# First batch of an attention, gated-MLP and expert kernel: three split products become one fp32 product, values before u, and the weights are split behind the norm

## The chip, the cores and the metric

The kernel runs on one core of a Trainium2 chip. The metric is the time of one execution on the device in microseconds; three runs of the kernel before gave 959.96, 960.23 and 961.21 us, the median is 960.23 us. The engines are TensorE (PE, whose weight loads are a row of their own, PEld), VectorE (DVE), ScalarE (ACT), GpSimd (POOL) and SyncE (SP, which here only issues DMA).

## The reference

Three layers stand one behind the other, for 8 batches of 576 rows: attention over keys and values that are averaged in groups of 8, a gated MLP, and two of four small attention experts for each row. The change touches the first batch of the first two. Cut to these:

```python
k_p = k.reshape(B, H, 72, 8, D).mean(axis=3)
v_p = v.reshape(B, H, 72, 8, D).mean(axis=3)
attn = softmax(q @ k_p.T / sqrt(D))
x = (attn @ v_p)                          # 8 heads side by side: 576 x 512
h = gelu(x @ w_in)                        # w_in: 512 x 1024
u, v = h[..., :512], h[..., 512:]
v_n = (v - mean(v)) / sqrt(var(v) + 1e-06) * g_ln
v_s = w_sg @ v_n + b_sg                   # over the 576 rows
x2 = x + (u * v_s) @ w_out
```

The weights w_in and w_out and all else are float32 in the reference; the kernel gets these two as pairs of 32-bit words of a 64-bit number, which it turns into float32 on the chip.

## The kernel before

The program has two phases, each a class. Phase A (`PhaseA`) does attention and gated MLP and stores x2 to DRAM in two parts, a high and a low one; phase B does the experts. The work of phase A goes batch by batch. Each batch has these steps: pooling of k and v (`pool_k`, `pool_v`), scores in five tiles of 128 rows (`score`), exponentials (`probs`), scaling by the sum (`finish`), transposes of the probabilities (`trans`), attention times values (`av`), copies of x out of PSUM (`put_x`), the v half of the MLP (`vpart`, in the first batch `vfirst` and one `vpart` for the last 64 rows), the norm of v (`norm`), the u half (`upart`, four blocks of 128), the spatial product over the rows (`spatial`, four blocks, each followed by the gate u * v_s) and the output product (`outp`, four blocks, which end in x2h and x2l and their stores).

Most products are made of three: both operands are split into a high part (float32r, a rounded float32) and a low part, and the sum is high x high + high x low + low x high. The scores and the transposes are plain float32 products (on PE they show as two records each for a product). The high parts are copies on ACT, the low parts subtractions on DVE or POOL.

The first batch also loads the weights. `load64` turns a staged block of w_in (`load_wi`, 8 blocks: parts 0 are u, parts 1 are v) or w_out (`load_wo`, 4 blocks) into a high and a low part, with two instructions on ACT and six on DVE (L124 to L130). The order of the first batch is written by hand: `SEQ` is a string of step names, and `first` calls them in this order (W and a number is `load_wi`, U is `upart`, Y is `vfirst`, V the last `vpart`, N the norm, S the spatial weights, O `load_wo`, P `spatial`; C, X and F are score, probabilities and scaling of the second batch, k its key pooling, v its value pooling). A scheduler below may interleave what is independent. Tables give the engine: `FD` lists the tiles (batch, tile) whose scaling runs on DVE, the others run on POOL; `SE` says for four spatial weight blocks whether D (DVE) or P (POOL) makes the low part. The output products of batch b are interleaved with the transposes of batch b + 1, and `av` of b + 1 follows them; behind it batch b + 1 begins with `vpart`.

Buffers are shared by tag: "raw" has three buffers, through which k, v and the staged w_out blocks go; "x2" has four, for the temporary tiles of `load64` and for x2h and x2l; "mm" has two PSUM buffers, for most products; "xg" has one, for the parts of x and then of the gate.

## Time and profile before

| what | value |
|---|---|
| median of three runs | 960.23 us |
| span of the profiled execution | 958.4 us |
| what the median run has more than the profiled span | 1.8 us |
| PE busy | 912.3 us (95%) |
| DVE busy | 693.4 us (72%) |
| ACT busy | 517.4 us (54%) |
| POOL busy | 445.2 us (46%) |
| PE busy from 132 us to the end | 813 of 826 us |
| second batch's first value product starts | 133.23 us |

The span runs from the first to the last instruction of the profiled execution; the profile gives no other time of it. Matmuls are pipelined: a record lasts longer than its distance from the next one, so prices on PE are read from start to start.

### The profile page before, as it was taken

How to read it: one execution, taken by the hardware profiler on the slowest of the kernel's cores; microseconds unless marked ns; L12 is line 12 of the kernel's file. 1: busy time of each engine (PE TensorE's matmuls, PEld its weight loads, DVE VectorE, ACT ScalarE, POOL GpSimd, SP SyncE). 2: the span in 40 equal slices, each digit the busy share in tenths (PEclk: the TensorE clock that was granted, in tenths of full speed). 3: DMA queues.
4: the chain of work that ended last, by engine and by line, in shares of the span. 5: the costliest groups of instructions: out<-in, count | busy, mean ns of one | idle time of the engine just before them, and what ended most of it. 6: DMA issues, size and time to landing. Idle time of an engine off the chain costs nothing.

```text
span 958.4 us, 18444 instructions
## 1 busy us (share of the span) xinstructions
PE 912.3 (95%) x6488; PEld 864.5 (90%) x6488; DVE 693.4 (72%) x1876; ACT 517.4 (54%) x1285; POOL 445.2 (46%) x621
## 2 busy tenths in 40 slices
PE   4897789999999999999999999899999999999997
PEld 4677769989989999899899899899999999999987
DVE  6998838667667577586576614897879797878785
ACT  3765324344343443343443433777777776877776
POOL 6554737658369368376583560122222222323221
PEclk9798989999999999999999999999999999999999
DMA  9601522312412404223116014425353534435121
GB/s 321 246 13 44 170 106 68 137 62 72 148 35 72 171 12 142 101 64 140 58 54 193 26 40 135 141 49 166 85 165 91 160 97 133 134 93 165 50 62 75
DMA packets 51644, 102.86 MB, mean 107 GB/s; under 512 B 10592, under 2 KB 16736, under 8 KB 50656
## 3 DMA queue, kind: packets, MB, share of 16 engines
q1 hardware_dynamic: 51408, 101.68, 33.1%
q8 instruction: 52, 0.85, 0.4%
q14 instruction: 40, 0.33, 0.1%
q10 hardware_dynamic: 144, 0.00, 0.0%
HBM read 59.72 MB, written 28.31 MB: 92 GB/s over the span
## 4 chain that ended last, share of the span: by engine, by line
PE 75%; DVE 14%; ACT 4%; issue 3%; DMA 2%; SPq 1%; POOL 1%; ACTq 0%; DVEq 0%; POOLq 0%
PE sc L224 4%; PE av L911 4%; PE op L457 3%; PE sp L433 3%; PE sp L434 3%; PE sp L432 3%; PE up L416 3%; PE up L418 3%; PE up L417 3%; PE op L458 3%; PE op L459 3%; PE vp L355 3%; PE vp L356 3%; PE vp L357 3%; PE t L891 2%
## 5 line engine op out<-in xcount | busy, mean ns | idle before, releaser
L865 POOL TENSOR_SCALAR pr<-pr,sm,gw 128x128 f32<-128x128 f32 (+3 forms) x119 | 72.2, 608 | 209.6 <-DVE sm L861 137.6
L849 ACT ACTIVATE pr<-s,sm 128x256 f32<-128x256 f32 (+4 forms) x160 | 83.0, 520 | 41.3 <-DVE sm L846 19.5
L432 PE MATMUL sp<-wsh,vnh 128*128 128x288 f32 x256 | 78.7, 308 | 3.9 <-ACT vnh L400 3.9
L457 PE MATMUL op<-g,woh 128*128 128x288 f32 x256 | 77.3, 306 | 3.9 <-DVE x2l L464 3.1
L416 PE MATMUL up<-x,wih 128*128 128x288 f32 x256 | 76.9, 300 | 1.4 <-ACT xu L324 1.4
L458 PE MATMUL op<-g,woh 128*128 128x288 f32 x256 | 76.2, 298 | 1.4 <-DVE g L445 1.4
L433 PE MATMUL sp<-wsh,vnl 128*128 128x288 f32 x256 | 76.9, 300 | 0.6 <-DVE vnl L402 0.6
L434 PE MATMUL sp<-wsl,vnh 128*128 128x288 f32 x256 | 76.8, 300 | 0.0
L418 PE MATMUL up<-x,wil 128*128 128x288 f32 x256 | 75.9, 296 | 0.7 <-DVE wil L130 0.7
L720 PE MATMUL pj<-xbh,wql 128*128 128x288 f32 x256 | 75.5, 295 | 0.0
L718 PE MATMUL pj<-xbh,wqh 128*128 128x288 f32 x256 | 75.5, 295 | 0.0
L719 PE MATMUL pj<-xbl,wqh 128*128 128x288 f32 x256 | 75.5, 295 | 0.0
L417 PE MATMUL up<-x,wih 128*128 128x288 f32 x256 | 75.1, 293 | 0.0
L459 PE MATMUL op<-g,wol 128*128 128x288 f32 x256 | 74.2, 295 | 0.0
L846 DVE CUSTOM_DVE_ANT_0 s<-s,mk 128x512 f32<-128x512 f32 (+3 forms) x128 | 62.3, 487 | 3.2 <-PE t L891 2.9
L896 DVE TENSOR_TENSOR pbl<-t,pbh 128x512 fp32r<-128x512 f32 (+3 forms) x128 | 60.4, 484 | 2.5 <-ACT pbh L895 0.9
L224 PE MATMUL sc<-kbd,qt 128*128 128x144 f32 (+1 forms) x320 | 50.7, 306 | 11.8 <-DMA qt<-q_in 8.3
L891 PE MATMUL t<-ident,pr 128*128 128x128 f32 x320 | 56.3, 277 | 3.3 <-POOL pr L865 3.1
L911 PE MATMUL av<-pbh,vt 128*128 128x320 f32 (+4 forms) x224 | 55.9, 279 | 2.7 <-ACT pbh L895 2.7
L224 PEld LDWEIGHTS sc<-kbd,qt 128*128 128x128 f32 (+1 forms) x320 | 44.7, 193 | 14.7 <-issue 11.1
L464 POOL TENSOR_TENSOR x2l<-x2l,x2h 128x576 fp32r<-128x576 f32 x8 | 11.4, 1428 | 99.1 <-ACT x2h L463 99.1
L400 ACT ACTIVATE vnh<-vg,rs 128x512 fp32r<-128x512 f32 (+1 forms) x40 | 27.2, 718 | 53.1 <-POOL rs L392 40.4
(247 smaller groups left out, 3352.1 us busy)
## 6 DMA issues: line engine op xcount, KB each, us to landing
kraw<-k_in SPq DMA_DIRECT2D x16, 576.0 KB, 3.8
x<-x2h SPq DMA_DIRECT2D x32, 288.0 KB, 2.1
x<-x2l SPq DMA_DIRECT2D x32, 288.0 KB, 2.1
xbl<-x SPq DMA_DIRECT2D x32, 288.0 KB, 4.1
xbh<-x SPq DMA_DIRECT2D x32, 288.0 KB, 3.9
kd<-scr SPq DMA_DIRECT2D x64, 144.0 KB, 2.5
out<-o SPq DMA_DIRECT2D x32, 288.0 KB, 4.1
vraw<-v_in SPq DMA_DIRECT2D x16, 512.0 KB, 4.0
```

The costliest lines, as they stand in the source:

```text
L224: nc.tensor.matmul(ps[:m, p // 2, (p % 2) * 144:(p % 2) * 144 + 144], qt[:, p, o:o + m], kbd[:, p, :], start=p % 2 == 0, stop=True, skip_g ...
L416: nc.tensor.matmul(o, self.wi[0][:, kc, c], xh, start=kc == 0, stop=False)
L417: nc.tensor.matmul(o, self.wi[0][:, kc, c], xl, start=False, stop=False)
L418: self.upmm = nc.tensor.matmul(o, self.wi[1][:, kc, c], xh, start=False, stop=kc == 3).ins
L432: nc.tensor.matmul(o, vh[:, k, c], self.ws[0][:, k, s], start=k == 0, stop=False)
L433: nc.tensor.matmul(o, vl[:, k, c], self.ws[0][:, k, s], start=False, stop=False)
L434: nc.tensor.matmul(o, vh[:, k, c], self.ws[1][:, k, s], start=False, stop=False)
L457: nc.tensor.matmul(o, self.wo[0][:, k, c], gh[:, s], start=k == 0, stop=False)
L458: nc.tensor.matmul(o, self.wo[0][:, k, c], gl[:, s], start=False, stop=False)
L459: self.opmm = nc.tensor.matmul(o, self.wo[1][:, k, c], gh[:, s], start=False, stop=k == 3).ins
L849: nc.scalar.activation(pt[:, s], o, AF.Exp, bias=st[:, 0:1], scale=-1.0, accum_out=st[:, 1 + 4 * j:2 + 4 * j])
L911: nc.tensor.matmul(ps[:, s - lo:], vt[:, j, 2 * p + e].rearrange("p a d -> p (a d)"), t[:, e, j * PTS + s:j * PTS + up], start=j == 0 and ...
```

## The change

In the first batch alone, x, v and u are computed by one float32 product each in place of three products of parts. The pooled v is kept as one float32 tile `v32` (in the buffer of the high part), the transposed probabilities as one tile, and x only as `XU` (no high or low part). `load64` now gives one float32 block, with one ACT instruction and three on DVE (L131 to L133). The second batch and later ones need the parts of w_in, so a new step D (`split_wi`: a copy on ACT, a subtraction on DVE) makes them behind the products' own loads and ahead of the norm in the list; for w_out the split stands inside `load_wo`. `parts_v` makes the two part tiles of v when the second batch pools. In `SEQ` the v weights and products (W4 Y0 to W7 Y3, V4) now stand ahead of the u ones (W0 U0 and on), and their staging h2 h3 ahead of h0 h1. `FD` gets three more tiles of the second batch, `SE` is all DVE, and two low parts of the gate go from POOL to DVE.

```diff
-FD = {(0, 0), (0, 1), (1, 3), (1, 4)}
+FD = {(0, 0), (0, 1), (1, 0), (1, 1), (1, 2), (1, 3), (1, 4)}
-SE = 'PDPP'
+SE = 'DDDD'
-       "s4 e4 f4 y0 y1 y2 t0 t1 t2 t3 t4 z l W0 U0 W1 U1 W2 U2 K Q k o0 o1 W4 Y0 W5 Y1 W6 Y2 W7 Y3 S2 S1 S0 "
-       "V4 W3 N0 U3 S4 N2 S5 N4 S3 C0 C1 o2 O0 P0 C2 X0 X1 F0 o3 O1 P1 C3 F1 X2 O2 R P2 F2 X3 O3 "
+       "f4 y0 y1 y2 t0 t1 t2 t3 t4 z l W4 Y0 W5 Y1 W6 Y2 W7 Y3 V4 W0 U0 W1 U1 N0 W2 U2 K Q k o0 o1 W3 "
+       "U3 N2 N4 S2 S1 S0 S4 S5 D4 D5 D6 D7 D0 D1 D2 D3 S3 C0 C1 o2 O0 P0 C2 X0 X1 F0 o3 O1 P1 C3 F1 X2 "
...
-        nc.scalar.activation(gf, zf, AF.Copy, scale=2.0 ** -112)
-        nc.vector.tensor_scalar(g, g, 3, 0x7FFFF000, op0=OP.logical_shift_left, op1=OP.bitwise_and)
-        nc.vector.scalar_tensor_tensor(a, zh, 0x80000000, g, op0=OP.bitwise_and, op1=OP.bitwise_or)
-        nc.scalar.activation(hi, a.bitcast(F32), AF.Copy)
-        nc.vector.tensor_scalar(g, a, 0xFF800000, None, op0=OP.bitwise_and)
-        nc.vector.tensor_scalar(zh, zh, 0x1FF, None, op0=OP.bitwise_and)
-        nc.vector.scalar_tensor_tensor(lf, zh, 2.0 ** 32, zl, op0=OP.mult, op1=OP.add)
-        nc.vector.scalar_tensor_tensor(lo, lf, 2.0 ** -52, gf, op0=OP.mult, op1=OP.mult)
+        nc.scalar.activation(g.bitcast(F32), zh.bitcast(F32), AF.Copy, scale=2.0 ** -112)
+        nc.vector.tensor_scalar(g, g, 3, None, op0=OP.logical_shift_left)
+        nc.vector.scalar_tensor_tensor(g, zl, 29, g, op0=OP.logical_shift_right, op1=OP.bitwise_or)
+        nc.vector.scalar_tensor_tensor(out.bitcast(U32), zh, 0x80000000, g, op0=OP.bitwise_and, op1=OP.bitwise_or)
+
+    def split(self, src, hi, lo, eng=None):
+        self.nc.scalar.activation(hi, src, AF.Copy)
+        (eng or self.nc.vector).tensor_sub(lo, src, hi.bitcast(F32))
...
         nc.scalar.activation(hi[:, :, o:o + m], ps[:, :, :m], AF.Copy)
+        if b == 0:
+            return
         nc.vector.tensor_sub(lo[:, 0:4, o:o + m], ps[:, 0:4, :m], hi[:, 0:4, o:o + m].bitcast(F32))
...
+            self.X32[b, p] = self.XU[b][:, p * S:p * S + S].rearrange("p (a n) -> p a n", a=2)
+            nc.scalar.activation(self.X32[b, p], ps[:, :, :HS], AF.Copy)
+            return
...
-            nc.tensor.matmul(ps, xh, wh, start=kc == 0, stop=False)
-            nc.tensor.matmul(ps, xl, wh, start=False, stop=False)
-            nc.tensor.matmul(ps, xh, wl, start=False, stop=kc == 3)
+            nc.tensor.matmul(ps, self.XU[0][:, o:o + 128], self.w32[:, kc, 512:], start=kc == 0, stop=kc == 3)
...
+                if b == 0:
+                    self.upmm = nc.tensor.matmul(o, self.w32[:, kc, c], self.X32[b, kc][:, h], start=kc == 0, stop=kc == 3).ins
+                    continue
...
-        eng = nc.vector if d >= (3 if b else 2) else nc.gpsimd
+        eng = nc.gpsimd if b and d < 3 else nc.vector
```

On PE, the first batch had its u products first (`up`, L416 to L418) and then the v products (`vp`, L371 to L373). Six rows where the one passes into the other:

```order
L416 MATMUL up<-x,wih 128x288
L417 MATMUL up<-x,wih 128x288
L418 MATMUL up<-x,wil 128x288
L371 MATMUL vp<-wih,x 128x512
L372 MATMUL vp<-wih,x 128x512
L373 MATMUL vp<-wil,x 128x512
```

On PE now, from the first batch's attention times values (`av`; the rows with `vl` are the narrow ones of the last 8 pooled keys) to the second batch's second score group (`sc`):

```order
L340 MATMUL av<-pth,v_99 128x288
L334 MATMUL av<-pth,vl_244 128x288 x7
L340 MATMUL av<-pth,v_99 128x288 x6
L417 MATMUL vp<-w_73,xu 128x512 x16
L256 MATMUL sc<-kbd,qt 128x144 x4
L386 MATMUL vp<-w_73,xu 64x512 x4
L460 MATMUL up<-xu,w_73 128x288 x32
L256 MATMUL sc<-kbd,qt 128x144 x4
```

The v products have moved ahead of all u products, each is one product, and the score groups have moved to either side of the u products.

On ACT now, around the last u blocks (`xu<-up` is a u block's gelu, `e,st<-sc,st` an exponential piece of the second batch's first tile):

```order
L467 ACTIVATE xu<-up 128x576
L266 ACT_TABLE_LOAD
L266 ACTIVATE e,st<-sc,st 128x72 x7
L467 ACT_TABLE_LOAD
L467 ACTIVATE xu<-up 128x576
L266 ACT_TABLE_LOAD
L266 ACTIVATE e,st<-sc,st 128x72
L136 ACTIVATE woh<-w_616 128x4x128
L467 ACT_TABLE_LOAD
L467 ACTIVATE xu<-up 128x576
L130 ACTIVATE g_681<-st_547 128x512
L277 ACT_TABLE_LOAD
```

Before, the four gelus of u stood ahead of the exponentials, with one table load between them; now the exponentials stand among them, with five.

On DVE now, behind the wait for those exponentials (`P` is the scaling of the second batch's first tile, `wol` the low part of an output weight block, `xu<-sp,xu` the gate product, `g<-xu,g` its low part):

```order
L286 RECIPROCAL st<-st 128x8
L289 TENSOR_TENSOR P<-e,st 128x512
L292 TENSOR_TENSOR P<-e,st 128x4x16 x2
L261 TENSOR_REDUCE st<-sc 128x8
L137 TENSOR_TENSOR wol<-w_616,woh 128x4x128
L269 TENSOR_TENSOR e<-sc,st 128x576
L131 TENSOR_SCALAR g_681<-g_681 128x512
L132 SCALAR_TENSOR_TENSOR g_681<-st_547,g_681 128x512
L133 SCALAR_TENSOR_TENSOR w_680<-st_547,g_681 128x512
L485 TENSOR_TENSOR xu<-sp,xu 128x576
L284 TENSOR_REDUCE st<-e 128x8
L261 TENSOR_REDUCE st<-sc 128x8
```

The scaling `P`, which was POOL's, now stands at the head of this stretch, ahead of the first gate product.

## Rows read from the trace of the kernel before

**Rows 1.** The page, part 1: busy us, share of the span, instructions

```profile
PE 912.3 (95%) x6488; PEld 864.5 (90%) x6488; DVE 693.4 (72%) x1876; ACT 517.4 (54%) x1285; POOL 445.2 (46%) x621
```

**Rows 2.** Stretches: us, busy us of each engine (instructions), granted clock, DMA share, GB/s

```profile
39.50:77.00 37.50, 31.13 (x180) 26.92 (x179) 35.43 (x66) 24.82 (x39) 16.25 (x9) 1.00 0.17 54
77.00:84.00 7.00, 6.31 (x25) 5.97 (x26) 5.84 (x13) 5.14 (x19) 0.00 (x0) 0.52 0.05 12
84.00:124.00 40.00, 30.50 (x223) 28.73 (x221) 32.80 (x59) 16.10 (x50) 27.11 (x36) 1.00 0.46 159
124.00:132.00 8.00, 7.44 (x36) 5.80 (x37) 2.58 (x7) 2.02 (x4) 1.98 (x2) 0.57 0.39 150
132.00:958.00 826.00, 813.20 (x5929) 778.03 (x5927) 586.58 (x1674) 451.96 (x1109) 371.34 (x523) 1.00 0.31 98
```

**Rows 3.** PE in order of time: start, us, instruction, idle before and releaser

```profile
41.77 0.40 PE L416 MATMUL up<-x,wih 128*128 128x288 f32 x1 [1.36 <-ACT xu L324]
...
51.39 0.39 PE L371 MATMUL vp<-wih,x 128*128 128x512 f32 x1
...
62.53 0.39 PE L344 MATMUL vp<-wih,x 128*128 128x512 f32 x1
...
76.39 0.53 PE L432 MATMUL sp<-wsh,vnh 128*128 128x288 f32 x2 [3.44 <-ACT vnh L400]
...
133.23 0.39 PE L355 MATMUL vp<-wih,x 128*128 128x512 f32 x1
```

**Rows 4.** The first scores on PE, and two pieces of the chain that ended last

```profile
15.26 5.29 PE L224 MATMUL sc<-kbd,qt 128*128 128x144 f32 x24 [1.69 <-issue]
...
15.26 4.18 PE sc L224 x16
...
85.76 0.99 PE sc L224 x8
```

**Rows 5.** DVE in order of time: one weight block after another

```profile
42.60 0.69 DVE L125 SCALAR_TENSOR_TENSOR a<-st,g 128x512 uint32<-128x512 uint32 x1
43.21 0.68 DVE L130 SCALAR_TENSOR_TENSOR wil<-st,g 128x512 fp32r<-128x512 f32 x1
...
44.48 0.42 DVE L124 TENSOR_SCALAR g<-g 128x512 uint32<-128x512 uint32 x1
44.82 0.68 DVE L129 SCALAR_TENSOR_TENSOR st<-st 128x512 f32<-128x512 uint32 x1
45.42 0.68 DVE L125 SCALAR_TENSOR_TENSOR a<-st,g 128x512 uint32<-128x512 uint32 x1
```

**Rows 6.** DVE by line, 20 to 106 us: busy us, mean ns, idle before

```profile
L277 DVE TENSOR_TENSOR ptl<-tr,pth 128x512 fp32r<-128x512 f32 (+1 forms) x5 | 3.1, 614 | 0.0
L321 DVE TENSOR_TENSOR x<-av,x 128x576 fp32r<-128x576 f32 x4 | 3.0, 750 | 0.3 <-ACT x L320 0.2
```

**Rows 7.** ACT in order of time: the table load ahead of the exponentials

```profile
79.89 1.28 ACT L234 ACT_TABLE_LOAD   x1
```

**Rows 8.** DVE in order of time, 84 to 106 us

```profile
84.47 0.76 DVE L438 TENSOR_TENSOR xu<-sp,xu 128x576 f32<-128x576 f32 x1 [1.56 <-PE sp L436]
...
103.09 1.48 DVE L257 TENSOR_TENSOR P<-e,st 128x512 f32<-128x512 f32 x1
104.50 1.27 DVE L445 TENSOR_TENSOR g<-xu,g 128x576 fp32r<-128x576 f32 x1
```

**Rows 9.** One stretch, columns as in group 2

```profile
85.00:105.00 20.00, 17.27 (x125) 15.94 (x123) 19.68 (x36) 11.56 (x43) 17.86 (x20) 1.00 0.21 73
```

**Rows 10.** The DMA queue and ACT in order of time, 115 to 123 us

```profile
115.35 0.33 SPq L71 DMA_DIRECT2D vraw<-v_in  x1
115.73 0.50 SPq L466 DMA_DIRECT2D x<-x2h  x1
...
122.69 0.65 ACT L463 ACTIVATE x2h<-op 128x576 fp32r<-128x576 f32 x1 [4.26 <-DMA x<-x2h]
```

**Rows 11.** Weight loads by line, 130 us to the end: busy us, mean ns

```profile
L416 PEld LDWEIGHTS up<-x,wih 128*128 128x128 f32 x224 | 42.2, 188 | 0.8
```

More of the change, by code (lines that the diff above doesn't have):

```diff
@@ L83, in consts @@
         nc.scalar.dma_start(self.cm, self.ins["cm"])
[L84 removed]
+        self.kbd, self.v32 = [], []
         for i in range(1):
[L86 to L88 removed]
+            for n, tag, sh in (("kbd", "kbd0", [128, NP, 144]), ("v32", "vhi0", [128, NP, 128])):
+                t = c.tile(sh, F32, tag=tag, name=n)
+                nc.gpsimd.memset(t, 0.0)
                 getattr(self, n).append(t)
@@ L96, in consts, with parts_v @@
         nc.gpsimd.memset(self.vn2[64:66].bitcast(F32), 1.0)
+    def parts_v(self):
+        self.vhi, self.vlo = [], []
+        for l in (self.vhi, self.vlo):
+            n = "vhi0" if l is self.vhi else "vlo0"
+            t = self.c.tile([128, NP, 128], F32R, tag=n, name=n)
+            self.nc.gpsimd.memset(t.bitcast(F32), 0.0)
+            l.append(t)
     def load_gln(self):
@@ L145, in load_wi, with split_wi @@
         k, s = self.wi_cols(part, i)
-        self.load64(self.STG.pop((part, i)), self.wi[0][:, k, s], self.wi[1][:, k, s])
+        self.load64(self.STG.pop((part, i)), self.w32[:, k, s])
+    def split_wi(self, part, i):
+        k, s = self.wi_cols(part, i)
+        self.split(self.w32[:, k, s], self.wi[0][:, k, s], self.wi[1][:, k, s])
     def stage_wo(self, f):
@@ L184, in pool_v @@
         raw = self.RAW["v", b]
+        if b == 0:
+            v = self.v32[0]
+            for i in parts:
+                t = raw[i]
+                eng = nc.vector if VE[b][i] == "D" else nc.gpsimd
+                eng.tensor_add(t[:, 0:4], t[:, 0:4], t[:, 4:8])
+                eng.tensor_add(t[:, 0:2], t[:, 0:2], t[:, 2:4])
+                if i < 2:
+                    for h in range(2):
+                        r = slice(64 * h, 64 * h + 64)
+                        eng.tensor_add(v[r, 2 * i:2 * i + 2, 64 * h:64 * h + 64], t[r, 0], t[r, 1])
+                    continue
+                eng.tensor_add(t[:, 2], t[:, 0], t[:, 1])
+                v1 = w.tile([128, 2, 64], F32, tag="vl1", name="vl0")
+                eng.tensor_mul(v1, t[:, 2, None, :].to_broadcast([128, 2, 64]), self.cm[:, 2:4, None].to_broadcast([128, 2, 64]))
+                self.KV[b] = (v, v1)
+            return
+        if b == 1:
+            self.parts_v()
         vhi, vlo = self.vhi[0], self.vlo[0]
@@ L268, in trans @@
         if i == 0:
-            self.PT[b] = [w.tile([128, 5, S], F32R, tag="pv", name=n, bufs=2) for n in ("pth", "ptl")]
-        hi, lo = self.PT[b]
+            self.PT[b] = [w.tile([128, 5, S], F32R if b else F32, tag="pv", name=n, bufs=2) for n in ("pth", "ptl")[:b + 1]]
+        hi, lo = self.PT[b] if b else self.PT[b] * 2
         p = self.P.pop((b, i))
@@ L292, in av @@
                 for h, s in enumerate(half):
-                    for st, mv in ((v2, lo), (v1, hi)):
+                    for st, mv in ((v2, lo), (v1, hi)) if b else ((v1, hi),):
                         for p in range(NP):
@@ L296, in av @@
                             mm(ps[p][:, h, :HS], st[r].rearrange("p a b -> p (a b)"), mv[r, 4, s],
-                               start=st is v2 and p not in done, stop=st is v1 and p in done, skip_group_check=True)
+                               start=(st is v2 or b == 0) and p not in done, stop=st is v1 and p in done, skip_group_check=True)
             else:
@@ L301, in av @@
                     first = "r" not in done
-                    mm(o, vhi[:, x], hi[:, x, s], start=first, stop=False, skip_group_check=True)
+                    mm(o, vhi[:, x], hi[:, x, s], start=first, stop=not b and not first, skip_group_check=True)
+                    if b == 0:
+                        continue
                     mm(o, vhi[:, x], lo[:, x, s], start=False, stop=False, skip_group_check=True)
@@ L311, in put_x @@
         nc, w = self.nc, self.w
+        if b == 0:
+            if b not in self.XU:
+                self.XU[b] = w.tile([128, 2368 * 2], F32, tag="xu", name="xu")
+            self.X32[b, p] = self.XU[b][:, p * S:p * S + S].rearrange("p (a n) -> p a n", a=2)
+            nc.scalar.activation(self.X32[b, p], ps[:, :, :HS], AF.Copy)
+            return
         if b not in self.XX:
@@ L340, in vpart @@
         self.LN[b, t0] = g
+        if b == 0:
+            for kc in range(4):
+                nc.tensor.matmul(ps[:m, 0], self.XU[0][:, kc * S + 512:kc * S + S], self.w32[:, kc, 512:], start=kc == 0, stop=kc == 3)
+            nc.scalar.activation(g[:m, 0], ps[:m, 0], AF.Gelu_apprx_tanh)
+            return
         if t0 == 4:
```

43 lines of the change are left out of this document (20 added, 23 removed), and 1 row of the table SEQ.

## Prediction

> **What bounds the kernel now.** I read the table of engines first, then the busy time by stage, then the order of time of each engine in the stages that lose. TensorE (PE) is busy 912 of 958 us [rows 1], so work taken off any other engine counts only where PE waits for it. The table by stage says where that is: from 132 us to the end PE is busy 813 of 826 us, but between 39.5 and 132 us it is not [rows 2]. From 39.5 to 77 us it misses 6.4 us, from 84 to 124 us 9.5 us, and in two stretches (77 to 84 and 124 to 132 us) it runs at a granted clock of 0.52 and 0.57, at the lower of its two levels for most of the time, each time after it had idled. These stretches are the first batch and the handing over to the second. VectorE (DVE) is busy 35.4 of 37.5 us and then 32.8 of 40 us there: it is the engine that PE waits for. All eight batches run one behind the other, and behind 132 us PE has next to no gap, so the whole change is read from one mark: the start of the second batch's first value product, now 133.23 us [rows 3]. What this mark gains, the end gains.
>
> **Price of the new products.** A full fp32 product is no new operation here: the scores are such products. Eight records (two for each product) of 144 columns take 0.99 us at full clock [rows 4], so a product takes 0.247 us, or 1.71 ns for a column. That gives 0.49 us for 288 columns and 0.875 us for 512. Now, three products stand in its place: 72 of 288 columns lie between 41.77 and 51.39 us, 0.134 us each, and 48 of 512 between 51.39 and 62.53 us, 0.232 us each [rows 3]; three cost 0.40 and 0.70 us. So PE gets more to do: 16 value products 14.0 for 11.1 us, the last 64 rows four for eight, 3.5 for 1.9 us, 32 u products 15.7 for 12.8 us: 7.4 us more, all of it in a stage where PE leads the path now.
>
> **The value stage up to 40 us.** The transposes wait for the normalised probabilities that GpSimd (POOL) makes last; nothing in that chain is removed but two steps of DVE, so av begins at about 31 us as now. It has 8 products of 288 columns, and 8 of 32 rows that run four beside each other, about 3 times the time of one; at the lower clock a product takes 0.98 us, so all would be 10.8 us. In the first scores of the trace 24 records of fp32 took 5.29 us together, but the first 16 of them 4.18 us and so the last 8 only 1.1 [rows 4]: their duration halved in the middle of a run of nothing but fp32 products. I take the same here, 4.2 us at the lower clock and the rest at the full one, 7.6 us in all: av ends near 39 us, now at 40.4 (1.36 us before 41.77) [rows 3]. A bound for the case that the narrow ones do not run beside each other is 3 us more.
>
> **PE from 39 to 74 us.** In the new order the values come first, then a score group (1.0 us), the last rows (3.5), all four u blocks (15.7) and another score group (1.0): 39 + 14.0 + 21.2 = 74.2 us. DVE must have the first four weight blocks by then. A block now takes six instructions, 2.82 us from one L125 to the next; those with three operands take 0.60 us from start to start, those with one operation 0.34 [rows 5]; behind the change three are left before the product, one of the single-operation kind and two of the three-operand kind, 1.54 us. Even if the first block starts at 26 us and the next wait for ScalarE (ACT) until 32 us, the eight are done at 44 us, and the v blocks by 37 us. The eight splits (0.6 us each), three of the four spatial differences from POOL and the first output block fit in before the values end at 53 us. So the norm runs from 53 to about 67 us under the u products, and its waits on POOL, for which PE stands idle now (3.4 us of idle time at 76.39 us alone [rows 3]), have PE's 21 us of u and scores as cover. Gone from DVE for good are the low parts of the transposes, 3.1 us, and of x, 3.0 us [rows 6], and 0.7 us for each of 12 weight blocks.
>
> **DVE from 74 us on.** Here DVE leads again, and here the change adds to it: the scaling of the second batch's first three probability tiles (0.86 + 2 x 0.3 us each) and two low parts of the gate (0.67 us each). The start is set by the exponentials of the second batch's first tile. They stand on ACT between the gelus of u blocks 1 and 3, with five table loads of 1.28 us [rows 7] among them, and end at about 74 us. From there to the last low part of the gate I count, with the spacings that DVE has when POOL is quiet: 4 scalings of 1.46 us, 4 gate products, 4 low parts and 4 maxima of 0.67, one difference and one sum of 0.67, 3 weight splits of 0.6, two weight blocks of 1.54 and ten small ones of 0.1: 21.1 us. POOL is not quiet: now, the 36 instructions from 84.47 us to the end of the low part at 104.50 us [rows 8] would take 16.3 us at those spacings and take 21.2, 1.30 times as long, with POOL busy 17.9 of 20 us [rows 9]. Behind the change POOL pools the second batch's v and the third's k there, some 17.7 of 26 us, three quarters of that share, so I take 1.23: 26.0 us, and the last low part is done at 100 us, now 105.8. Bounds are 1.0 (POOL in the way of nothing) and 1.44 (each instruction with two inputs in SBUF pays what L257 and L445 pay at 103 and 104.5 us, 0.6 us over their 0.86 and 0.67).
>
> The Trainium skill ("SBUF — State Buffer", section "Who interferes with whom") says the same of the kind of instruction: one with two SBUF inputs contends with a GpSimd instruction that reads SBUF, one with at most one does not. The trace agrees: the gate product L438, with one input in PSUM, takes 0.76 us where L445 takes 1.27 [rows 8]. By that rule 1.44 would be nearer, since scalings, low parts and splits are all of that kind, and the mark would come 4.4 us later; the measured stretch had such instructions as well, which is why I stay at 1.23.
>
> **From the gate to the mark.** Now this takes 27.4 us (105.8 to 133.2). Of this, PE's own work is the last 14 products of the first output block (1.9 us), three more blocks of 24 (9.5), four groups of transposes (1.9) and the second batch's av, 28 product times with a wait for the last transpose (4.7): 18 us. The other 9.4 us are the lower clock and one wait: the third x2h needs the buffer of the first, whose store was issued at 115.73 us and landed for ACT at 122.69 us, 7 us later [rows 10]. It went out late because the queue stood behind a load of v that waited for POOL to pool k until 115.35 us. Behind the change that POOL chain starts earlier: the raw buffer of an output block is free after its third instruction, not its sixth, and POOL has no scalings and no low part of the gate before it. Following the buffers, POOL ends with k at about 99 us, so load of v and q go out before the first store is ready at 103 us; the 1.7 MB before it need some 5 us, it lands near 107 us, and the third x2h would not want it before 109. So the wait is hidden, by about 2 us only, and PE has no gap long enough to lose its clock. The mark comes at 100 + 18 = 118 us.
>
> **The sum.** 133.2 - 118 = 15 us less: the profiled execution's 958.4 us become 943.4; the median run is 1.8 us longer than the profiled span, 960.2, so 945 us. A change under 0.2% (1.9 us) could not be told from none.
>
> **Rivals.** (a) DVE is held by POOL at 1.44, and the store is late as well: the mark is at 122.5 us from the first alone (949.5 us); with the full 7 us for the store and the 10.5 us that now follow it, at 126 us, 953 us. For it speaks that q, 1.2 MB, is queued directly ahead of the stores; against it that POOL loses three scalings. (b) DVE is not held: 95 + 18 = 113 us, 940 us. Against it stands the 1.30 measured. (c) Slower: the clock does not hold through the fp32 products. If all of the 35 us from 39 to 74 us ran at the lower level, the mark would be at 153 us and the time 980 us; from 15 us at that level on the change loses. Against it: the score groups at full clock [rows 4], and PE without a gap. (d) Also not faster: the weight loads of fp32 products show. There are two for each product, on 52 products from 39 to 74 us, and at 0.188 us (what a load of the u products now lasts, under a product) [rows 11] this is 19.6 us: no gain, 5 us lost. Against it: the score records of 0.124 us hold their loads too. The Trainium skill ("TensorE: Matmul & The Clock Gate", section "Weight-path perf modes — Fast Weight Load (FWL) and DoubleRow") speaks for it: fast weight load is not used for FP32. By it only the loads grow; the score records, two 144-column passes each, leave nothing for them to show.
>
> **Chances.** Forecast (gain 12 to 18 us) 0.62; more (b) 0.12; less than 12 us (a) 0.19; no change from several small waits 0.03; slower (c, d) 0.04. So faster 0.93, same 0.03, slower 0.04. The range takes in (b) with 1 us and (a) with its second case: 939 to 953 us.
>
> **What will show it.** Right: records of the u products 0.245 us apart at clock 1.00; values before u, ending near 53 us; spatial products starting at 74 to 75 us with no wait for the norm; DVE full from 74 to 100 us; the first store landing before the third x2h asks; no drop of the clock near the second av; the mark at 118 us. Wrong would be: longer fp32 records, a PE gap before the spatial products, DVE waiting for ACT past 74 us, or the third x2h still waiting for a store.

## The result

The changed kernel takes 951.45 us (median of four executions, 949.94 to 952.18), the kernel before in the same comparison 960.39 us (959.96 to 961.21). The ratio is 0.9902, 95% interval 0.9885 to 0.9920: 8.9 us faster, where 15 were forecast. The profiled execution of the changed kernel has a span of 950.4 us (it is the one of 952.18 us, the slowest of the four), forecast 943.4.

The page of the changed kernel, part 1, answers to [rows 1]: busy us, share of the span, instructions.

```profile
PE 916.2 (96%) x6432; PEld 856.4 (90%) x6432; DVE 681.1 (72%) x1847; ACT 519.7 (55%) x1284; POOL 421.2 (44%) x599
```

PE is busy 3.9 us longer and the time falls: the gain is idle time and lower clock that are gone. The stretches of the changed kernel, columns as in [rows 2], the last two from the mark (121.6 us) to the end of phase A and from there to the end:

```profile
39.50:54.00 14.50, 14.29 (x36) 6.63 (x37) 14.43 (x26) 10.75 (x18) 0.22 (x1) 1.00 0.26 91
54.00:75.00 21.00, 20.24 (x78) 13.48 (x76) 14.59 (x28) 13.85 (x31) 5.79 (x6) 1.00 0.15 51
75.00:100.00 25.00, 22.69 (x158) 22.06 (x158) 23.21 (x41) 15.09 (x47) 17.20 (x23) 0.93 0.29 100
100.00:118.00 18.00, 16.08 (x118) 14.74 (x116) 14.20 (x29) 6.73 (x11) 1.50 (x4) 1.00 0.54 196
...
121.60:572.40 450.80, 449.64 (x3152) 424.02 (x3150) 292.83 (x495) 179.00 (x259) 279.73 (x381) 1.00 0.26 89
572.40:950.40 378.00, 365.15 (x2768) 354.86 (x2768) 295.56 (x1179) 272.38 (x850) 90.90 (x143) 0.99 0.37 109
```

The same last two of the kernel before, from its mark on:

```profile
133.20:584.00 450.80, 449.71 (x3152) 424.20 (x3150) 290.60 (x494) 178.80 (x258) 279.53 (x380) 1.00 0.26 89
584.00:958.40 374.40, 362.29 (x2768) 352.64 (x2768) 295.10 (x1180) 272.30 (x850) 90.92 (x142) 1.00 0.38 110
```

From 39.5 to 75 us PE is busy 34.5 of 35.5 us at full clock. From the mark to the end of phase A both kernels take 450.8 us for the same 3152 records of PE. Phase B takes 378.0 for 374.4 us: 3.6 us of what the mark had gained are lost 450 us later.

PE of the changed kernel in order of time, as in [rows 3]: the values, the last rows, u, the second batch's second score group with its wait, the first output product's low part, the mark.

```profile
39.71 14.00 PE L417 MATMUL vp<-w,xu 128*128 128x512 f32 x32 [0.65 <-ACT xu L356]
53.55 1.14 PE L256 MATMUL sc<-kbd,qt 128*128 128x144 f32 x8
54.62 3.65 PE L386 MATMUL vp<-w,xu 128*64 128x512 f32 x8
58.20 4.15 PE L460 MATMUL up<-xu,w 128*128 128x288 f32 x16
...
76.33 1.55 PE L256 MATMUL sc<-kbd,qt 128*128 128x144 f32 x8 [2.09 <-ACT e L266]
...
102.51 0.40 PE L505 MATMUL op<-g,woh 128*128 128x288 f32 x1 [0.40 <-DVE g L492]
...
121.64 0.40 PE L403 MATMUL vp<-wih,x 128*128 128x512 f32 x1
```

The mark came at 121.64 us: 11.6 us gained there, 15.2 forecast. PE had its u blocks done at 74.24 us (76.33 less the wait), 1.0 us behind the forecast, whose 74.2 has the second score group in it; then it waited 2.09 us for exponentials on ACT, and the spatial products began at 77.5 us, not at 74 to 75. Behind that wait PE ran at the lower level of its clock: its products are 0.24 us apart up to 80.6 us and 0.13 us from there on, which is the 0.93 of the third stretch. DVE waited for the same exponentials and began its stretch there:

```profile
76.31 0.19 DVE L285 TENSOR_SCALAR st<-st 128x8 f32<-128x8 f32 x1 [5.17 <-ACT e L266]
...
101.70 0.76 DVE L492 TENSOR_TENSOR g<-xu,g 128x576 fp32r<-128x576 f32 x1
```

So there are three places to explain: the exponentials (2.3 us late), the way from the last gate low part (102.5 us) to the mark, 19.2 for 18 us, and phase B (3.6 us).

### The profile page after: what moved, and what is told of

Read it like the earlier page. It is cut to its first block, busy times and chain, and to the rows that moved or that the text cites. A ratio compares the mean times of both kernels' runs of the same rounds, so it can differ in the third digit from the quotient of the medians.

```text
span 950.4 us, 18277 instructions
## 1 busy us (share of the span) xinstructions
PE 916.2 (96%) x6432; PEld 856.4 (90%) x6432; DVE 681.1 (72%) x1847; ACT 519.7 (55%) x1284; POOL 421.2 (44%) x599
## 4 chain that ended last, share of the span: by engine, by line
PE 77%; DVE 11%; ACT 5%; issue 3%; DMA 2%; SPq 1%; POOL 1%; ACTq 0%; DVEq 0%; POOLq 0%
PE sc L256 4%; PE op L504 4%; PE av L958 4%; PE op L505 4%; PE op L506 3%; PE sp L479 3%; PE sp L481 3%; PE sp L480 3%; PE up L463 3%; PE up L465 3%; PE up L464 3%; PE vp L405 3%; PE vp L403 3%; PE vp L404 3%; PE t L938 2%
## 5 line engine op out<-in xcount | busy, mean ns | idle before, releaser
L463 PE MATMUL up<-x,wih 128*128 128x288 f32 x224 | 67.2, 300 | 0.0
L465 PE MATMUL up<-x,wil 128*128 128x288 f32 x224 | 66.1, 295 | 0.0
L464 PE MATMUL up<-x,wih 128*128 128x288 f32 x224 | 65.6, 293 | 0.0
```

Of the source, the lines that this page charges most:

```text
L463: nc.tensor.matmul(o, self.wi[0][:, kc, c], xh, start=kc == 0, stop=False)
L464: nc.tensor.matmul(o, self.wi[0][:, kc, c], xl, start=False, stop=False)
L465: self.upmm = nc.tensor.matmul(o, self.wi[1][:, kc, c], xh, start=False, stop=kc == 3).ins
```

## The experiments

All start from the changed kernel but `order_only`, which starts from the kernel before. The gate is the end of its last low part, the mark as in the prediction, the rest the span less the mark, all in us of the profiled execution; the ratio is to the kernel before. `pool_quiet` leaves work out and is no kernel to use.

| kernel | median us | ratio, 95% interval | gate | mark | rest |
|---|---|---|---|---|---|
| before | 960.39 | 1 | 105.8 | 133.2 | 825.2 |
| changed | 951.45 | 0.9902 (0.9885 to 0.9920) | 102.5 | 121.6 | 828.8 |
| exps_together | 950.53 | 0.9907 (0.9885 to 0.9930) | 103.5 | 124.1 | 828.3 |
| pool_quiet | 946.70 | 0.9862 (0.9836 to 0.9887) | 97.6 | 117.0 | 825.3 |
| u_first | 957.64 | 0.9976 (0.9960 to 0.9992) | 110.7 | 130.7 | 826.9 |
| fill | 949.65 | 0.9890 (0.9869 to 0.9911) | 102.5 | 121.7 | 824.7 |
| order_only | 963.05 | 1.0025 (1.0011 to 1.0038) | 105.1 | 133.8 | 825.7 |
| scal_pool | 949.57 | 0.9887 (0.9866 to 0.9909) | 101.2 | 120.3 | 825.1 |
| gate_pool | 953.17 | 0.9915 (0.9900 to 0.9931) | 102.6 | 125.3 | 826.5 |
| exps_fill | 949.73 | 0.9876 (0.9856 to 0.9896) | 97.8 | 121.6 | 826.1 |
| exps_stores | 946.45 | 0.9855 (0.9816 to 0.9894) | 98.5 | 118.0 | 826.8 |
| stores_only | 950.39 | 0.9902 (0.9866 to 0.9938) | 102.7 | 121.9 | 828.6 |
| exps_stores_scal | 952.93 | 0.9930 (0.9906 to 0.9954) | 103.2 | 125.0 | 827.4 |
| var_dve | 949.08 | 0.9887 (0.9867 to 0.9907) | 101.9 | 121.1 | 825.4 |

### The two halves of the change alone: u_first and order_only

```diff
-SEQ = ("a0 a1 b0 d0 b3 b1 b2 d1 b4 d2 c g p0 h2 h3 p1 h0 h1 s0 e0 f0 s1 e1 f1 s2 s3 e2 f2 e3 f3 s4 e4 "
-       "f4 y0 y1 y2 t0 t1 t2 t3 t4 z l W4 Y0 W5 Y1 W6 Y2 W7 Y3 V4 W0 U0 W1 U1 N0 W2 U2 K Q k o0 o1 W3 "
+SEQ = ("a0 a1 b0 d0 b3 b1 b2 d1 b4 d2 c g p0 h0 h1 p1 h2 h3 s0 e0 f0 s1 e1 f1 s2 s3 e2 f2 e3 f3 s4 e4 "
+       "f4 y0 y1 y2 t0 t1 t2 t3 t4 z l W0 U0 W1 U1 W2 U2 K Q k o0 o1 W4 Y0 W5 Y1 W6 Y2 W7 Y3 V4 W3 N0 "
```

> The changed kernel with the order of before: three u blocks ahead of the values, single products and late splits kept. Theory (the order is what hides the norm): PE ends its last u block at about 74 us but the norm, which begins only behind the values at about 70 us, ends 10 to 14 us later, so PE waits 6 to 10 us ahead of the spatial products, at 80 to 84 us, and the clock falls behind that; the mark comes at 129 to 135 us, 958 to 964 us: the single products alone gain nothing. Rival (DVE's work is the bound and the order matters little, since the late splits and the output blocks fill DVE while PE makes u): the mark moves by less than 3 us, 951 to 954 us.

PE of u_first at the first spatial products:

```profile
80.27 0.61 PE L479 MATMUL sp<-wsh,vnh 128*128 128x288 f32 x1 [5.68 <-ACT vg L387]
...
84.89 0.61 PE L479 MATMUL sp<-wsh,vnh 128*128 128x288 f32 x1 [2.81 <-ACT vnh L444]
```

PE waits 8.5 us for the norm and what stands behind it on ACT, and from 86 to 110 us the mean granted clock is 0.85. The mark is at 130.7 us: the single products with the old order gain 2.5 us there, as the theory had it. But the old order alone doesn't make the whole wait. ACT, which made PE wait the first 5.68 us, had itself waited for POOL, and POOL pooled the second batch's v and the third batch's k without a pause from 61.2 us until it came to the norm's addition:

```profile
77.34 0.23 POOL L435 TENSOR_SCALAR rs<-mv 128x2 f32<-128x2 f32 x1
```

```profile
78.40 1.33 ACT L444 ACTIVATE vnh<-vg,rs 128x512 fp32r<-128x512 f32 x2 [11.39 <-POOL rs L436]
```

DVE had the statistics for it ready at 66.8 us. In the kernel before and in the changed one this pooling comes behind the norm; in the kernel before, with the same order of PE, PE waited 3.44 us at that product [rows 3]. So this run does not price the order by itself: the place of the pooling on POOL came with it, and no run parts the two.

The opposite: the `SEQ` of the change without its D steps, in the kernel before, all else as it was.

```diff
-       "s4 e4 f4 y0 y1 y2 t0 t1 t2 t3 t4 z l W0 U0 W1 U1 W2 U2 K Q k o0 o1 W4 Y0 W5 Y1 W6 Y2 W7 Y3 S2 S1 S0 "
-       "V4 W3 N0 U3 S4 N2 S5 N4 S3 C0 C1 o2 O0 P0 C2 X0 X1 F0 o3 O1 P1 C3 F1 X2 O2 R P2 F2 X3 O3 "
...
+       "f4 y0 y1 y2 t0 t1 t2 t3 t4 z l W4 Y0 W5 Y1 W6 Y2 W7 Y3 V4 W0 U0 W1 U1 N0 W2 U2 K Q k o0 o1 W3 "
+       "U3 N2 N4 S2 S1 S0 S4 S5 S3 C0 C1 o2 O0 P0 C2 X0 X1 F0 o3 O1 P1 C3 F1 X2 "
```

> The kernel before with the order of the change alone: values, then the last rows, then u; three products each, weights split ahead of their products as before, scalings and gate low parts on POOL as before. Theory (the gain is the norm's waits hidden under u; the single products serve to take the six-instruction weight blocks and low parts off DVE ahead of the values): PE makes the values at the pace of DVE's weight blocks, 2.8 us each, and u at that pace too, with the norm between them on DVE, so the spatial products start at 77 to 80 us (changed kernel 77.4) and the mark comes at 124 to 129 us for 133.2, 951 to 956 us. Rival 1 (the order is the whole of it): the mark comes at 119 to 122 us and the time is no more than the changed kernel's. Rival 2 (without the single products the order gains nothing): the mark stays above 131 us, 958 to 962 us.

The theory's place was right (spatial products from 79.5 us), its mark was not: rival 2. PE waits within u, on the weight blocks:

```profile
65.75 0.40 PE L416 MATMUL up<-x,wih 128*128 128x288 f32 x1 [2.67 <-ACT wih L126]
...
67.72 0.61 PE L418 MATMUL up<-x,wil 128*128 128x288 f32 x1 [1.44 <-DVE wil L130]
```

The norm is hidden, but the weight blocks that DVE has to split ahead of each product are not, DVE is full from 79 to 110 us (29.6 of 31 us busy), and from the gate to the mark nothing changes (28.7 us, before 27.5). So one half of the change (with the moves between engines, `FD`, `SE` and the low parts) gains 2.5 us at the mark and the other loses 0.6, but both together gain 11.6. The table parts that sum at the gate: 3.3 us are gained ahead of it and 8.3 behind it, 19.2 us for 27.5. The way behind it is short in `u_first` too (20.0 us) and not in `order_only`, where the third x2h waits for the first store again, 1.91 us, and PE's clock is 0.79 from 110 to 134 us: these 8.3 us come with the single products and the moves between engines, not with the order. Ahead of the gate neither half gains much alone: the order 0.7 us, with the waits above for its weights; the single products lose 4.9, with the norm and the pooling that `u_first` has ahead of it.

### What DVE's stretch is made of: pool_quiet, scal_pool, gate_pool

In `pool_k`, and then in `pool_v`:

```diff
+            if b == 2:
+                self.nc.gpsimd.tensor_add(t[:, 0, 0, 0:4], t[:, 0, 0, 0:4], t[:, 4, 0, 0:4])
+                continue
...
+            if b == 1:
+                nc.gpsimd.tensor_add(t[:, 0, 0, 0:4], t[:, 0, 0, 0:4], t[:, 4, 0, 0:4])
+                continue
```

> The changed kernel without the pooling of the second batch's v (the 128-row parts) and of the third batch's k on POOL; two small additions stand in its place, so these values are left out of the result. Theory (DVE's 26.1 us from 76.3 to 102.4 us are 21.1 us of work held up 1.23 times by POOL): the stretch falls to 21 to 22.5 us, the last gate low part ends at 98 to 99 us, the mark is at 117.5 to 118.5 us, 947.5 to 948.5 us. Rival (the stretch is set by PE's spatial products, which DVE waits for): the means of the DVE rows fall, idle time of DVE grows in their place, and the mark moves by less than 1 us.

DVE, first and last row of the stretch and the scaling and low part between (L295 and L498 here are L289 and L492 of the changed kernel):

```profile
76.60 0.17 DVE L291 TENSOR_SCALAR st<-st 128x8 f32<-128x8 f32 x1 [5.16 <-ACT e L272]
77.05 0.69 DVE L295 TENSOR_TENSOR P<-e,st 128x512 f32<-128x512 f32 x1
81.64 0.75 DVE L491 TENSOR_TENSOR xu<-sp,xu 128x576 f32<-128x576 f32 x1
83.64 0.75 DVE L498 TENSOR_TENSOR g<-xu,g 128x576 fp32r<-128x576 f32 x1
...
96.84 0.75 DVE L498 TENSOR_TENSOR g<-xu,g 128x576 fp32r<-128x576 f32 x1
```

And the same three instructions in the changed kernel, with POOL at its pooling:

```profile
76.77 1.05 DVE L289 TENSOR_TENSOR P<-e,st 128x512 f32<-128x512 f32 x1
82.89 0.76 DVE L485 TENSOR_TENSOR xu<-sp,xu 128x576 f32<-128x576 f32 x1 [0.27 <-PE sp L483]
84.89 1.25 DVE L492 TENSOR_TENSOR g<-xu,g 128x576 fp32r<-128x576 f32 x1
```

With POOL quiet the stretch takes 21.0 us (76.60 to 97.59, of which 0.54 us are a wait for ACT), with the pooling 26.1 (76.31 to 102.46): the count of 21.1 and the factor of 1.23 both hold (1.24 measured), and the mark moves by 4.6 us with it. The gate product, with one input in PSUM, takes the same in both. The Trainium skill ("SBUF — State Buffer", section "Who interferes with whom") says that a DVE instruction with two inputs in SBUF contends with a POOL instruction that reads SBUF and that one with at most one input there, outside the 2-port modes that the section names, does not; these rows agree.

```diff
-FD = {(0, 0), (0, 1), (1, 0), (1, 1), (1, 2), (1, 3), (1, 4)}
+FD = {(0, 0), (0, 1), (1, 3), (1, 4)}
```

> The changed kernel with the scalings of the second batch's first three probability tiles back on POOL, as before. Theory (DVE is the bound from 76 to 102 us and each instruction on it is lengthened by what POOL does): DVE loses three groups of about 1.9 us, POOL gets three of about 3 us ahead of or between its pooling, which ends 6 to 9 us later; the first transposes wait for POOL, the first store lands late, and the mark moves to 122 to 125 us, 951.5 to 955 us. Rival (only DVE's own count matters): the gate ends 4 to 5 us earlier and the mark is at 117 to 118 us, 947 to 948 us.

Neither. The mark comes 1.3 us earlier, not later: DVE is relieved (gate at 101.2), and POOL ends later without holding the transposes up. This part of the change doesn't pay by itself. The interval of the ratio overlaps that of the changed kernel, so it is the trace that says it, not the time.

```diff
-        eng = nc.gpsimd if b and d < 3 else nc.vector
+        eng = nc.vector if d >= (3 if b else 2) else nc.gpsimd
```

> The changed kernel with the low parts of the gate's first two blocks back on POOL, as before. Theory (POOL is in the middle of pooling v when they come, and its queue is in order): they wait behind an instruction or a load there, PE's output block isn't held by them before 101 us, POOL ends its k 3 us later, and the mark stays within 1 us of 121.6, 950.5 to 952.5 us. Rival (DVE's count): DVE loses 2 us in its stretch and the mark comes at 119.5 to 120 us, 949.5 us.

The first half of the theory is right and its size wrong. PE:

```profile
102.65 0.61 PE L505 MATMUL op<-g,woh 128*128 128x288 f32 x1 [2.96 <-POOL g L492]
```

The second low part stands behind POOL's pooling and comes at 102.6 us; PE, which was waiting, then runs at the lower level of its clock, and the mark is 3.7 us later. The move of the low parts to DVE is worth that much, though it lengthens DVE's stretch.

### The late exponentials: exps_together, exps_fill, var_dve

The first tile's eight exponentials behind the gelu of u block 1, and the gelu of block 2 behind the last of them:

```diff
-       "f4 y0 y1 y2 t0 t1 t2 t3 t4 z l W4 Y0 W5 Y1 W6 Y2 W7 Y3 V4 W0 U0 W1 U1 N0 W2 U2 K Q k o0 o1 W3 "
-       "U3 N2 N4 S2 S1 S0 S4 S5 D4 D5 D6 D7 D0 D1 D2 D3 S3 C0 C1 o2 O0 P0 C2 X0 X1 F0 o3 O1 P1 C3 F1 X2 "
+       "f4 y0 y1 y2 t0 t1 t2 t3 t4 z l W4 Y0 W5 Y1 W6 Y2 W7 Y3 V4 W0 U0 W1 U1 N0 K Q k C0 W2 U2 o0 o1 W3 "
+       "U3 N2 N4 S2 S1 S0 S4 S5 D4 D5 D6 D7 D0 D1 D2 D3 S3 C1 o2 O0 P0 C2 X0 X1 F0 o3 O1 P1 C3 F1 X2 "
...
+            with self.tc.issue_after(self.gelu) if (b, i) == (1, 0) else nullcontext():
+                for h in range(8):
...
+        with self.tc.issue_after(self.exp) if (b, f) == (0, 2) else nullcontext():
             self.gelu = nc.scalar.activation(u, ps[:, :, :HS], AF.Gelu_apprx_tanh).ins
```

> The changed kernel with the eight exponentials of the second batch's first probability tile in one run on ACT, between the gelus of u blocks 1 and 2, so that three table loads stand there for five. Theory (what came 2.3 us later than forecast is DVE waiting for these exponentials): the last of them ends at 72.8 to 73.5 us instead of 76.2, PE's wait of 2.09 us before the second score group goes, DVE starts its stretch about 3 us earlier, the mark (first value product of the second batch) comes at 118.5 to 119.5 us instead of 121.6, and the median falls from 951.45 to about 949. Rival (PE's 21 us of scores and spatial products, or POOL's pooling, set the end of the gate as much as DVE does): the wait goes, but the last gate low part stays at 101.5 to 102.4 and the mark at 121 to 122 us, 951 us.

PE's wait of 2.09 us went and the exponentials ended at 74.6 us, but DVE did the second output block's split and the third block ahead of the second score tile (its maximum at 81.36 for 78.56 us), and a new wait came:

```profile
83.63 1.61 PE L256 MATMUL sc<-kbd,qt 128*128 128x144 f32 x8 [2.94 <-DVE e L270]
```

The mark was later, 124.1 us: the gate came 1.0 us later, and from 105 to 110 us PE's granted clock was 0.68. A second try holds these two on DVE until that tile's difference is done (and has the doubled transposes of the next section):

```diff
+        with self.tc.issue_after(self.sub) if f == 2 else nullcontext():
             self.load64(self.STG.pop((2, f)), t)
+        with self.tc.issue_after(self.sub) if f in (1, 2) else nullcontext():
             self.split(t, self.wo[0][:, :, c], self.wo[1][:, :, c])
```

> The exponentials together again, now with the second output weight block's split and the third block held on DVE until the second score tile's difference is done (what came ahead of that difference in the first try made PE wait 2.9 us), and with the 15 transposes made twice, so that the late fall of the clock stays away. Theory (the exponentials' end sets DVE's start): DVE starts at 74.7 us for 76.3, PE has no wait over 1 us before the gate, the last gate low part ends at 99.5 to 101 us, the mark is at 119 to 120.3 us, the rest takes 825 us: a span of 944 to 945.5 us, a median of 946 to 948 us. Rival (another wait takes the place of the exponentials, as it did): the mark stays at 121 us or later, 949.5 us.

Both the theory and its rival: the gate ended at 97.8 us, 4.6 us earlier and better than forecast, and the mark stayed at 121.6. ACT, and the stretch behind it:

```profile
110.92 0.65 ACT L514 ACTIVATE x2h<-op 128x576 fp32r<-128x576 f32 x1 [1.77 <-DMA x<-x2h]
```

```profile
108.00:113.00 5.00, 3.77 (x31) 3.56 (x30) 2.69 (x5) 1.36 (x2) 0.00 (x0) 1.00 0.90 351
113.00:118.00 5.00, 5.00 (x29) 3.55 (x28) 0.96 (x3) 1.49 (x3) 1.40 (x1) 0.62 0.51 196
118.00:123.00 5.00, 5.00 (x25) 4.75 (x25) 3.23 (x7) 2.80 (x5) 3.54 (x3) 0.70 0.00 0
```

The third x2h waits for the first store. This is the wait of [rows 10], which the prediction had hidden "by about 2 us only": a gate 4.6 us earlier used the cover up. The store stood on the queue right behind the load of q, which had come behind the v load that waited for POOL:

```profile
102.59 0.42 SPq L65 DMA_DIRECT2D qt<-q_in  x1
103.07 0.42 SPq L517 DMA_DIRECT2D x<-x2h  x1
```

It landed 7.7 us after its issue; in the changed kernel, issued at 106.49 us, it took 3.0. PE idled 1.2 us ahead of the next transposes, and its clock fell to the lower level behind that.

Why the exponentials were late at all was asked with one instruction moved:

```diff
-        nc.gpsimd.tensor_scalar(rs[:m, 0, :n], mv[:m, :n, 1], 1e-6, None, op0=OP.add)
+        (nc.gpsimd if b else nc.vector).tensor_scalar(rs[:m, 0, :n], mv[:m, :n, 1], 1e-6, None, op0=OP.add)
```

> The changed kernel with the one small addition of the first batch's norm (variance plus constant, 128x2) on DVE, not on POOL. There, for tiles 2 and 3, it took 2.60 us at 60.86 us where the same one takes 0.63 in the kernel before, ACT stood 4.04 us for what follows it, and the gelus and the second batch's first exponentials stand behind that on ACT. Theory (that is why the exponentials ended at 76.2 us and not at the forecast 74): ACT's wait ends near 62.3 us for 64.3, the last exponential ends at 74.0 to 74.5 us, PE's second score group waits under 0.5 us, the last gate low part ends at 100 to 100.7 us, the mark is at 119.3 to 120.3 us; median 949 to 950 us where the late fall of the clock comes in some executions as it did. Rival (the five table loads around the gelus set the end of the exponentials, since the eighth waits for the gelu of u block 2 anyway): the wait on ACT shrinks, the eighth exponential still ends above 75.5 us, and the mark stays at 121 to 122 us.

The theory fell: ACT's wait is still 3.79 us (it was 4.04), the mark 0.5 us earlier. POOL of the changed kernel, and then of this one:

```profile
60.86 2.60 POOL L435 TENSOR_SCALAR rs<-mv 128x2 f32<-128x2 f32 x1 [2.45 <-DVE mv L434]
63.54 0.71 POOL L436 TENSOR_TENSOR rs<-rs,mhalf 128x2 f32<-128x2 f32 x1
```

```profile
61.64 2.53 POOL L436 TENSOR_TENSOR rs<-rs,mhalf 128x2 f32<-128x2 f32 x1 [3.08 <-DVE rs L435]
```

Now the power takes the 2.5 us that the addition took; with DVE idle the two took 0.23 and 0.71 us (`u_first`, 77.34 and 77.66 us). In both kernels the instruction of POOL that comes there ends only about when three DVE instructions with two inputs in SBUF (two of L439 and one of L176, done at 63.4 us in the one kernel and 63.6 in the other) are over. That these three are what holds it was read from the order of time, not tested. By that reading DVE holds POOL here; in the stretch behind it POOL holds DVE, as `pool_quiet` shows. The Trainium skill says in the same place ("SBUF — State Buffer", section "Who interferes with whom") that issue order decides who blocks; by the recorded starts these rows don't bear it out, since the addition began at 60.86 us and the first of the three at 61.26.

### The loss in phase B: fill

The changed kernel at the start of phase B, three stretches, and the kernel before 11.6 us later:

```profile
592.40:596.40 4.00, 3.56 (x25) 2.76 (x23) 3.83 (x14) 2.68 (x9) 0.00 (x0) 1.00 0.70 180
596.40:600.40 4.00, 1.90 (x10) 1.22 (x9) 3.55 (x15) 2.66 (x9) 1.65 (x3) 0.87 0.95 269
600.40:606.40 6.00, 5.93 (x27) 5.91 (x28) 3.68 (x22) 1.84 (x8) 1.24 (x3) 0.52 0.83 264
```

```profile
604.00:608.00 4.00, 3.58 (x26) 2.87 (x24) 3.83 (x14) 2.66 (x9) 0.00 (x0) 1.00 0.70 174
608.00:612.00 4.00, 1.72 (x11) 1.12 (x9) 3.55 (x15) 2.82 (x9) 1.57 (x3) 1.00 0.87 212
612.00:618.00 6.00, 5.85 (x45) 5.77 (x46) 5.53 (x27) 4.13 (x14) 1.31 (x3) 1.00 0.88 305
```

The instructions and waits are the same (transposes that wait for probabilities from POOL), and PE is as empty; but in the one execution the clock fell behind it, for 27 instructions in 6 us in place of 45, in the other not.

```diff
-                for j in range(j0, j1):
+                for j in [*range(j0, j1)] * (2 if (b, p) == (0, 0) else 1):
...
-            for j in range(i + 1):
+            for j in [*range(i + 1)] * (2 if (b, p) == (0, 0) and u < 5 else 1):
```

> The changed kernel with the first batch's 15 first transposes of the second stage made twice, to the same place, so that PE has more to do in the stretch from 592 to 601 us where it waits for probabilities. Behind the mark the changed kernel loses 3.6 us that the kernel before doesn't: 828.8 for 825.2 us from the mark to the end. Theory (the clock falls to the lower level from 599 to 606 us because PE is half idle ahead of it): with the fuller stretch the clock stays, the mark stays at 121.6 and the rest takes 825 to 826.5 us, 948 to 949.5 us. Rival (the fall of the clock has to do with something else there, such as the DMA at 0.95): it stays, and the time is 951.5 to 953 us.

```profile
596.40:600.40 4.00, 3.14 (x24) 2.52 (x22) 3.88 (x19) 2.94 (x10) 1.22 (x2) 1.00 0.93 242
600.40:606.40 6.00, 5.57 (x45) 5.37 (x44) 4.90 (x25) 4.03 (x15) 1.66 (x3) 1.00 0.92 294
```

The clock stays at a DMA share as high as in the changed kernel, and the rest takes 824.7 us. But the other kernels say more: without the doubled transposes the fall was there in three of ten profiled executions (changed, exps_together, stores_only; their rests are the three above 828 us), with them in none of four. And var_dve, whose mark is 0.5 us from that of the changed kernel, didn't have it. If the fall comes in three of ten whatever the transposes do, four without it have a chance of one in four (0.7 to the fourth power is 0.24), so it isn't shown that the doubled transposes keep it away. The loss in the profiled execution is shown, 3.6 us against the kernel before (the rests without the fall lie between 824.7 and 827.4 us); in the three executions with the fall PE was busy 1.9 to 2.1 of the 4 us ahead of it, but in the seven without it 1.6 to 2.2, so a half empty PE alone doesn't decide it; that the change brings it is not shown. It comes in some executions of the same instructions, and what decides is open. By the medians, fill is 1.8 us below the changed kernel, about half of that loss, which is less than the spread within either.

### A faster version: exps_stores, stores_only, exps_stores_scal

The loads of the third batch's v and q go behind the second output block's stores. `exps_stores` has this on top of the edits of exps_fill, `stores_only` has it alone, and `exps_stores_scal` is `exps_stores` with the `FD` of `scal_pool`:

```diff
                 self.load_k(n + 1)
-                self.load_v(n + 1, 0)
-                self.load_q(n + 1)
+                if b:
+                    self.load_v(n + 1, 0)
+                    self.load_q(n + 1)
...
                 self.outp(b, f)
+                if (b, f) == (0, 1):
+                    with self.tc.issue_after(self.store):
+                        self.load_v(2, 0)
+                        self.load_q(2)
```

> The kernel with the exponentials together and the doubled transposes, with one edit more: the loads of the third batch's first v part and of its q go out behind the second output block's stores, not ahead of the first. Theory (with the exponentials together the gate ends at 97.8 us, but the queue then stood behind a v load that waited for POOL's k until 102.6 us, so that the third x2h waited 1.8 us for the first store, PE 1.2 us for the transposes, and the clock fell): the first store goes out at 101.9 us, the third x2h has no wait, the clock stays, and the mark comes at 116.5 to 117.5 us, 18.5 to 19.5 us behind the gate; span 941.5 to 943 us, median 944 to 946 us. Rival (the delayed v load holds the second batch up in turn, or the transposes' wait has another cause): the mark stays above 119 us.

The store goes out at 102.52 us, the third x2h has no wait for it, and the granted clock is 1.00 from 75 to 130 us:

```profile
109.70 0.65 ACT L514 ACTIVATE x2h<-op 128x576 fp32r<-128x576 f32 x1
```

```profile
118.01 0.40 PE L406 MATMUL vp<-wih,x 128*128 128x512 f32 x1
```

The mark is at 118.0 us, 19.5 us behind the gate, and 946.45 us is the fastest time of a kernel that computes the whole: 14 us below the kernel before, 5 below the changed one (each compared with its own runs of the kernel before, 960.50 and 960.39 us). The intervals of the two ratios just touch; against `stores_only`, run beside it, the executions don't overlap (944.37 to 948.45, 948.53 to 952.61 us). Of the 5 us the mark has 3.6; the rest may be the doubled transposes. The forecast of 118 us thus comes true with two waits taken away that it had not seen or had thought hidden, but by luck as well: the gate is 1.5 us earlier than forecast (98.5 for 100) and the way from there 1.5 us longer (19.5 for 18).

> The changed kernel with that last edit alone: the third batch's v and q loads behind the second output block's stores. Theory (in the changed kernel the first store lands before the third x2h needs its buffer, so nothing waits for it): the mark stays at 121 to 122 us and the time within 1 us of 951.45 us, less only where the late fall of the clock stays away. Rival (stores hold up something here that shows no wait, such as the DMA engines' share): the mark moves by more than 1 us.

The stores alone give nothing (mark 121.9, 950.39 us): in the changed kernel the store was in time.

> The first kernel of this set, with the scalings of the second batch's first three probability tiles back on POOL as well. In the changed kernel this gained 1.3 us at the mark. Theory (once the exponentials are together PE, with 21 us of scores and spatial products from 75 us on, is the bound as much as DVE): nothing gained, the mark within 0.5 us of the first kernel's or later, since POOL ends its k later. Rival (DVE is the bound still): the mark comes 1 to 3 us earlier, 114 to 116 us.

Worse than both theories: POOL, with the scalings, has the last of them late, DVE waits 3.81 us for it ahead of the last tile's maximum, and the last low part stands behind that:

```profile
103.21 0.61 PE L509 MATMUL op<-g,woh 128*128 128x288 f32 x1 [4.11 <-DVE g L496]
```

Of the 7.0 us at the mark 4.7 are at the gate; the other 2.3 come behind it, where PE's granted clock was 0.58 from 105 to 110 us. So where the scalings belong depends on what else is at its place: on POOL in the changed kernel (1.3 us), on DVE once the exponentials are together (7 us).

## Why the prediction was right, and where it was short

The time is inside the range, and faster was given 0.93, but the gain is 8.9 us for 15: it lies where the range had been drawn wide for rival (a), and its mechanism is not that one: DVE was held by 1.23 and not 1.44, and the store was in time. The mark, 11.6 us gained for 15.2, is what the prediction's mechanism has to answer for. Two of its own signs of being wrong came, a PE gap before the spatial products and DVE waiting for ACT past 74 us; both are the late exponentials.

- **Price of the products, values, u**: right. 32 records of the values take 14.0 us, the last rows 3.6 for 3.5, u 16.0 for 15.7; av ended at 39.1 us, and the values began 0.7 us later than the sum has it. No weight load shows and the clock holds, so rivals (c) and (d) are out.
- **"They ... end at about 74 us"** (the exponentials): failed, 76.2 us. The five table loads were counted; the wait of ACT for the norm's reciprocal root on POOL, 4.04 us ahead of the gelus, was not. The prediction gave the norm's waits "PE's 21 us of u and scores as cover". PE had that cover; ACT, whose list has the gelus and the exponentials behind that wait, had none. 2.3 us. That the wait accounts for them is read from ACT's order of time: no run took it away (3.79 us were left in var_dve), and in exps_together the exponentials ended at 74.6 us with a wait of 4.63, since two table loads and a gelu fewer stood ahead of the last one. The place of the eighth exponential could be named as the cause as well.
- **21.1 us times 1.23**: right in both factors (21.0 and 26.1 us measured, 1.24).
- **From the gate to the mark, 18 us**: too small, 19.2 us; 19.2 to 19.5 in scal_pool, pool_quiet and exps_stores too, at the full clock. The second batch's av took 5.4 us for 4.7 (116.27 to 121.64), the three output blocks 9.9 for 9.5; the transposes took their 1.9. 1.2 us.
- **The store hidden by about 2 us**: hidden, as forecast, and by more: it landed 3.0 us after 106.49 us and the third x2h asked at 113.35, 3.9 us later. That this cover is needed is shown by taking it away (exps_fill) and giving it back (exps_stores).
- **"What this mark gains, the end gains"**: failed for this execution. It holds to 0.1 us to the end of phase A, but phase B lost 3.6 us to a lower clock. The prediction read the mean granted clock of 1.00 from 132 us on [rows 2] as a property of the kernel; it was one of that execution.

2.3 + 1.2 + 3.6 = 7.1 us, and the span is 7.0 us above the forecast. The last of the three is chance as far as is known: seven of ten such executions didn't have it.

## What to carry to other kernels

When a wait is moved under another engine's work, list what stands behind it on every engine that takes part in it: here PE was covered and ACT was not. Two edits of which each alone gains little or loses can gain much together, when one makes the room that the other fills, so measure the pair before calling either useless. When one of them is put back for a test, look at what else moved with it on every engine: in `u_first` it was POOL's pooling. After each wait taken away look at the next one with the smallest cover: it is the one that turns up.

## What the runs showed of the hardware

- DVE's 21.0 us became 26.1 while POOL pooled, shown by taking the pooling away. The other way, read from the order of time only, a POOL addition of 128x2 elements took 2.60 us, for 0.23 with DVE idle (`u_first`), while DVE ran three instructions with two SBUF inputs.
- The lower level of PE's clock came behind a stretch in which PE was busy 1.90 of 4 us in the changed kernel, which lost 3.6 us there, and not behind 1.72 of 4 us with the same instructions in the kernel before; it came in three of ten profiled executions with that stretch.
